# Row maxima of an attention block: their transposition, their store and one activation placed elsewhere

## The chip, the cores and the metric

The kernel runs on one core of one Trainium2 chip. The metric is the device time of one execution in microseconds (us); lower is better. The core has five engines with an instruction queue each: TensorE (PE, matrix products, results in PSUM; its weight loads are listed apart as PEld), VectorE (DVE), ScalarE (ACT), GpSimd (POOL) and SyncE (SP, which here only issues transfers, DMAs). A queue is worked off strictly in order: while an instruction waits for its operands, everything behind it on that engine waits too.

## What is computed

One transformer block on 2048 tokens of width 576: an attention with 32 heads of width 18 and a sliding window of 256 keys, then a shifted mixing layer and an MLP of inner width 4608. The change touches only the attention stage; there the output projection and the two normalizations that follow it are computed as well.

```python
h = layernorm(x) * (1 + ca) + sa
q, k, v = heads(h @ wqkv)                      # 32 heads of 18
scores = where(mask, q @ k.T * 18 ** -0.5, -1e9)   # mask: 0 <= i - j < 256
p = softmax(scores)
x = x + ga * ((p @ v) @ wo)
h = layernorm(x) * (1 + cb) + sb
x = x + gb * B(h)                              # B begins with layernorm(h) @ w1
```

## The kernel before

**Units.** The attention stage works in 32 units n = 0..31. Unit n belongs to 512 queries (group g = n // 8) and to two pairs of heads (j = 0, 1); its queries lie in one of four buffers `QD`, its keys in one of three buffers `KD`. Every unit passes two stations:

- *Maxima.* `mx` (L519 to L525) multiplies the queries with the keys of their window, on PE, in eight blocks of two 320-wide pieces; `red` (L534 to L541) takes the negative maximum of each row, on DVE, into `m`. When all eight blocks are through, `mtr` (L543) transposes `m` on PE into a PSUM tile `mt`, `mev` (L547) copies it to SBUF as `ms` on ACT, and `mst` (L551) stores it by two small DMAs into rows 108 and 109 of the unit's query buffer. From then on the query buffer carries the maxima as two more rows, and the next station subtracts them inside its matrix product.
- *Scores.* About one unit later `xm` (L568, L570) computes the scores X on PE, ten tiles a unit (`X{n}_{j}_{k}`), and `ex` (L585) takes the exponential on ACT into P. Each unit therefore needs its two rows of maxima before its first X tile.

After every second unit comes the *value burst* `av` (L607): 208 small matrix products on PE, without a break, for a pair of units u. Its two results in PSUM are copied by ACT (`avs`, L612), transposed by PE (`ot`, L617) and divided by DVE (L624, L625). From unit 12 on, `wotile` weaves the output projection of one 128-token tile t into each pair of units: `wo` on PE (L692), a normalization on DVE and POOL (`ln1`, `ln2`), and at its end `ln2n` (L713), one activation on ACT that writes the normalized rows `xn`. Three stores by SP follow (`st1`, `st2`, `st3`: `xp`, `hbd`, `xnd`).

**PSUM banks.** Tiles carry a tag that names their bank. X tiles alternate between the banks s0 and s1; `av` and `ot` use s2 and s3; the `mx` blocks alternate between m0 and m1. A tile can be written only when the last reader of the tile before it in the same bank is done. The transposed maxima `mt` use s3.

**Order.** Nothing is scheduled automatically. Every step is entered with a time by `at(time, function)`, where `tm(h)` turns units into time (one unit is 13 of those), and at the end all steps are sorted by that time and issued; each engine's queue is the sorted list of the steps that use it. So a smaller number puts a step further ahead in its engine's queue, and the number has no other meaning. The steps that matter here stand in `wotile` (`ln2n` at h + 2.05) and in the loop over units (`mtr` at n + 1.16 for even n and n + 1.47 for odd n, `mev` .005 and `mst` .006 later). The burst `av` of the units 2u and 2u + 1 has the time 2u + 4.10, `avs` 2u + 4.41, `ot` 2u + 4.51.

**Queues of DMAs.** All large transfers are issued by SP. In the attention stage these are, for each unit, three loads for QD and three for KD, and for each pair of units the loads `or`, `xr` and V and the stores `od`, `xp`, `hbd`, `xnd`. Only the stores of the maxima are issued by ACT.

Of the kernel before, what the change touches and what calls it, by code (L numbers as in the profile page):

```python
# [8 lines left out]
F32 = mybir.dt.float32  # L9
# [10 lines left out]
P = 128  # L20
# [13 lines left out]
class Kern:  # L34
# [34 lines left out]
    def at(self, t, f, *a):  # L69
        self.ev.append((t, (lambda: f(*a)) if a else f))  # L70
# [382 lines left out]
    def attention(self, t1, t2, TA, HU, LX=2.05):  # L453
        nc, at, ps = self.nc, self.at, self.ps
        X, M = {}, self.rowm
        tm = lambda h: TA + HU * h
# [84 lines left out]
                    nc.vector.tensor_reduce(out=m[:, c + s:c + s + 1], in_=pm[:, s, 320 - w:320], axis=mybir.AxisListType.X, op=ALU.max, negate=True)  # L541

        def mtr(n):  # L543
            pt = X["mt", n] = ps.tile([16, P], F32, tag="s3", name=f"mt{n}")
            nc.tensor.transpose(pt, X["m", n], self.ident)

        def mev(n):  # L547
# [3 lines left out]
        def mst(n):  # L551
            ms, Q = X["ms", n], X["Q"][n % 4]
            for r in range(2):
                nc.scalar.dma_start(Q[108 + r:109 + r].bitcast(F32), ms[:, 64 * r:64 * r + 64].bitcast(F32))

        BANKS = [[(0, 0), (5, 320)], [(-2, 0), (1, 192)], [(-4, 0), (2, 64), (6, 384)], [(-3, 0), (3, 128), (7, 448)], [(-1, 0), (4, 256)]]

# [170 lines left out]
        def wotile(t, h, b0=2):  # L728
            at(tm(h - 0.2), orow, t)
            at(tm(h + 0.42), otT, t, b0)  # L730
            at(tm(h + 0.43), otev, t)
            at(tm(h + 0.77), wom, t, 0, b0)
            at(tm(h + 0.92), woe, t, 0)
            at(tm(h + 1.15), wom, t, 1, b0)
            at(tm(h + 1.16), ln1, t, 0)
            at(tm(h + 1.30), woe, t, 1)
            at(tm(h + 1.31), ln1, t, 1)
            at(tm(h + 1.95), st1, t)
            at(tm(h + 1.712), ln1n, t)
            at(tm(h + 1.714), ln2, t)  # L740
            at(tm(h + 2.05), ln2n, t)
            at(tm(h + 2.1), st2, t)
            at(tm(h + 2.35), st3, t)

        N = 32
        for n in range(N):
            at(max(t1 + .5 + n * .01, tm(n - (0.98 if n < 12 else 0.86))), load, n)
            for j in range(2):
                at(max(t1 + .6, tm(n - 0.3 + 0.5 * j)), qs, n, j)
                for bb in range(4):  # L750
                    th = n + (4 * j + bb) / 8
                    at(tm(th), mx, n, j, bb)
                    at(tm(th + .06), red, n, j, bb)
                    if n in (1, 2):
                        at(tm(th + .01), self.warm, 2, "s3")
                at(max(t2 + .01, tm(n + LX - (0.77 if n < 12 else 0.6) + 0.47 * j)), ks, n, j)
                for k in range(5):
                    th = n + LX + (5 * j + k) / 10
                    at(tm(th), xm, n, j, k)
                    at(tm(th + .03), ex, n, j, k)  # L760
            hm = n + (1.47 if n % 2 else 1.16)
            at(tm(hm), mtr, n)
            at(tm(hm + .005), mev, n)
            at(tm(hm + .006), mst, n)
        for u in range(16):
            h = 2 * u + LX + 2
            if u == 15:
# [14 lines left out]
        for t in range(10):  # L782
            wotile(t, 12.4 + 2 * t)
# [618 lines left out]
```

## Time and profile before

| what | value |
|---|---|
| median of 3 runs | 1792.72 us (1791.35 to 1794.88) |
| the profiled execution | 1794.32 us |
| its span, first to last instruction | 1792.5 us |
| mean granted clock of TensorE | 0.982 |
| stage of the projections of q, k and v | up to about 205 us of the span |
| attention stage | about 205 to 665 us |
| mixing layer, then MLP | from about 665 us to the end |

The span is the time between the first and the last instruction of the profiled execution. "Busy" is the time in which an engine works on instructions; "idle before" is the time that it stood still just before an instruction, with the engine and instruction that ended the wait behind the arrow. An idle time matters for the total only if the waiting engine is the one that sets the pace of the stage.

### The profile page before, as it was taken

The page shows a single profiled execution, that of the slowest core. Times are in us where ns is not written, and L with a number is a line of the kernel's source. Part 1 is how long each engine was busy: PE and PEld are TensorE (multiplying, and loading weights), DVE is VectorE, ACT ScalarE, POOL GpSimd, SP SyncE. Part 2 cuts the span into 40 slices and gives each one's busy share as a digit, 9 for nine tenths or more (in the row PEclk, how much of TensorE's full clock was granted, in tenths as well). Part 3 has the DMA queues.
Part 4 walks back from the last instruction along what each step waited for, and adds up shares of the span by engine and source line. Part 5 has one row for each costly group of instructions (what it writes and reads, how often), then busy time and mean ns, then how long its engine had stood idle before and what let it go on. Part 6 is the DMA issues. An engine that isn't in the chain of part 4 may idle for free.

```text
span 1792.5 us, 33622 instructions
## 1 busy us (share of the span) xinstructions
PE 1687.1 (94%) x13369; PEld 1535.6 (86%) x13369; DVE 1103.0 (62%) x1887; ACT 707.3 (39%) x1211; POOL 898.8 (50%) x837
## 2 busy tenths in 40 slices
PE   7999998999999989988799999999979999999998
PEld 5888887888989879988588999999878999999997
DVE  6544354666767636666666666666675666666664
ACT  3222144454545554444333433333433333344331
POOL 4222347445454533454766555556644556655550
PEclk9999998999999999999899999999989999999999
DMA  8854553546455446544422222211233211122211
GB/s 257 275 183 154 176 159 103 145 135 172 130 153 163 145 138 204 192 159 141 162 75 63 63 63 62 59 45 52 62 126 96 63 52 49 56 63 62 62 45 53
DMA packets 156499, 206.77 MB, mean 115 GB/s; under 512 B 19316, under 2 KB 87924, under 8 KB 155768
## 3 DMA queue, kind: packets, MB, share of 16 engines
q1 hardware_dynamic: 153720, 203.19, 36.9%
q8 instruction: 106, 1.74, 0.4%
q10 hardware_dynamic: 2624, 1.45, 0.3%
q14 instruction: 49, 0.40, 0.1%
HBM read 143.76 MB, written 60.56 MB: 114 GB/s over the span
## 4 chain that ended last, share of the span: by engine, by line
PE 73%; DVE 6%; DMA 5%; POOL 5%; issue 4%; ACT 4%; SPq 1%; ACTq 1%; POOLq 0%; DVEq 0%
PE d L1256 24%; PE qk L331 6%; PE X L568 3%; PE v L369 3%; PE mx L519 3%; PE wo L692 3%; PE av L607 3%; PE pg L916 2%; PE X L570 1%; PE w L965 1%; DVE W L1114 1%; DMA wmf<-in_w_mod_dram 1%; DMA or<-od 1%; DMA wf<-in_B_w_dram 1%; ACT avs L612 1%
## 5 line engine op out<-in xcount | busy, mean ns | idle before, releaser
L1256 PE MATMUL d<-W,G 128*128 128x288 f32 x3456 | 507.7, 297 | 12.5 <-DVE acc L1264 9.2
L1256 PEld LDWEIGHTS d<-W,G 128*128 128x128 f32 x3456 | 489.2, 189 | 34.9 <-DVE acc L1264 10.3
L1264 DVE TENSOR_TENSOR acc<-d,acc 128x576 f32<-128x576 f32 x288 | 216.9, 754 | 205.6 <-PE d L1256 203.2
L1094 POOL TENSOR_TENSOR wf<-wf 128x384 f32<-128x384 f32 x140 | 147.0, 1071 | 339.8 <-DMA wf<-in_B_w_dram 333.8
L585 ACT ACTIVATE P<-X 128x512 f32<-128x512 f32 (+4 forms) x320 | 177.8, 572 | 202.3 <-PE X L570 160.8
L537 DVE TENSOR_REDUCE m<-mx 128x2 f32<-128x640 f32 x144 | 117.8, 819 | 109.0 <-PE mx L523 108.5
L568 PE MATMUL X<-QD,KS 128*128 128x64 f32 (+2 forms) x704 | 146.2, 300 | 10.8 <-ACT P L585 9.8
L1106 POOL TENSOR_TENSOR W<-wf,W 128x768 fp32r<-128x768 f32 x70 | 152.9, 2207 | 1.2 <-ACT W L1100 1.2
L519 PE MATMUL mx<-KD,QS 128*128 128x320 f32 (+4 forms) x512 | 144.7, 342 | 7.4 <-DVE m L537 3.2
L1233 DVE TENSOR_TENSOR G<-U,G 128x512 fp32r<-128x512 f32 x108 | 88.5, 819 | 99.0 <-ACT G L1226 99.0
L499 POOL TENSOR_SCALAR QS<-QD,rowm 128x512 fp32r<-128x512 f32 x128 | 87.9, 701 | 111.6 <-DMA QD<-qd 56.4
L1224 ACT ACTIVATE U<-U 128x512 f32<-128x512 f32 x108 | 68.3, 632 | 178.3 <-DVE U L1209 178.2
L1224 ACT ACTIVATE C<-C 128x512 f32<-128x512 f32 x36 | 22.8, 632 | 286.4 <-DVE C L1209 286.4
L568 PEld LDWEIGHTS X<-QD,KS 128*128 128x128 f32 x704 | 108.6, 194 | 19.5 <-ACT P L585 16.1
L331 PE MATMUL qk<-hT,Wqk 128*128 128x512 f32 x462 | 109.3, 396 | 1.2 <-DVE qs L345 1.2
L506 POOL TENSOR_SCALAR KS<-KD,rowm 128x768 fp32r<-128x768 f32 (+1 forms) x128 | 108.5, 863 | 0.0
L1120 POOL TENSOR_TENSOR wf<-wf,gb 128x1152 f32<-128x1152 f32 x35 | 103.4, 2955 | 6.9 <-DMA wf<-in_B_w_dram 6.9
L331 PEld LDWEIGHTS qk<-hT,Wqk 128*128 128x128 f32 x462 | 86.4, 188 | 23.4 <-DVE qs L345 1.6
L519 PEld LDWEIGHTS mx<-KD,QS 128*128 128x128 f32 x512 | 93.5, 194 | 14.1 <-issue 5.3
L1135 POOL TENSOR_TENSOR W<-wf,W 128x1152 fp32r<-128x1152 f32 x35 | 96.8, 2766 | 6.9 <-ACT W L1129 6.9
L1100 ACT CAST W<-wf 128x1152 fp32r<-128x1152 f32 x70 | 90.2, 1318 | 20.5 <-DMA wf<-in_B_w_dram 10.4
L570 PE MATMUL X<-Mk,identr 128*128 128x256 f32 (+2 forms) x320 | 96.6, 302 | 0.0
(787 smaller groups left out, 3211.3 us busy)
## 6 DMA issues: line engine op xcount, KB each, us to landing
wf<-in_B_w_dram SPq DMA_DIRECT2D x35, 576.0 KB
wf<-in_B_w_dram SPq DMA_DIRECT2D x140, 128.0 KB
KD<-kd SPq DMA_DIRECT2D x72, 216.0 KB
QD<-qd SPq DMA_DIRECT2D x96, 144.0 KB
wf<-in_B_w_dram SPq DMA_DIRECT2D x140, 64.0 KB
qd<-qs SPq DMA_DIRECT2D x16, 512.0 KB
kd<-qs SPq DMA_DIRECT2D x16, 512.0 KB
vd<-Vst SPq DMA_DIRECT2D x16, 312.0 KB
```

The source lines that it names most:

```text
L331: nc.tensor.matmul(po, W[:, a, fs], H[:, c, :], start=(n == 0), stop=(n == 13))
L506: nc.gpsimd.tensor_scalar(t[:, b0:, r], src[:, b0:], M[:, 2 + r:3 + r], 0.0, op0=ALU.mult, op1=ALU.add)
L519: nc.tensor.matmul(pm[:, s, 320 - 64 * nb:320], lhs, K[:, j, 64 * (i + 5 - nb):64 * (i + 5)], start=True, stop=merged(n, j, bb))
L537: nc.vector.tensor_reduce(out=m[:, c:c + 2], in_=pm[:, :, 0:320], axis=mybir.AxisListType.X, op=ALU.max, negate=True)
L568: nc.tensor.matmul(px[:, c:c + q1 - q0], K[:, b + 4].rearrange("p r k -> p (r k)"), Q[:, j, q0:q1], start=(i == 0), stop=False)
L570: nc.tensor.matmul(o, self.identr, mv, start=False, stop=True)
L585: nc.scalar.activation(p[:, lo:], X["px", n, j, k][:, lo:], AF.Exp, scale=SCALE)
L1094: nc.gpsimd.tensor_tensor(out=WF[:, o], in0=WF[:, a], in1=WF[:, b], op=ALU.subtract)
L1106: eng.tensor_tensor(out=W[:, s0:s1, 3:5, :], in0=WF[:, 1 + s0:1 + s1, 0:2], in1=W[:, s0:s1, 0:2, :].bitcast(F32), op=ALU.subtract)
L1120: nc.gpsimd.tensor_tensor(out=R4, in0=R4, in1=gb.unsqueeze(1).to_broadcast([P, 2, D]), op=ALU.mult)
L1256: nc.tensor.matmul(po, G[:, g, ta, b, ts], W[:, w, b, cs], start=(n == 0), stop=(n == 5))
L1264: nc.vector.tensor_tensor(out=a, in0=po, in1=a, op=ALU.add)
```

## The change

There are three edits. The transposition `mt` of odd units moves from n + 1.47 to n + 1.105, which is directly behind the value burst (2u + 4.10 with n = 2u + 3), and its PSUM bank becomes s0 instead of s3. The two stores of the maxima are issued by SP instead of ACT, for all units, and .14 behind the transposition instead of .006. The activation `ln2n` moves from h + 2.05 to h + 1.86.

```diff
         def mtr(n):
-            pt = X["mt", n] = ps.tile([16, P], F32, tag="s3", name=f"mt{n}")
+            pt = X["mt", n] = ps.tile([16, P], F32, tag="s0" if n % 2 else "s3", name=f"mt{n}")
             nc.tensor.transpose(pt, X["m", n], self.ident)
...
             for r in range(2):
-                nc.scalar.dma_start(Q[108 + r:109 + r].bitcast(F32), ms[:, 64 * r:64 * r + 64].bitcast(F32))
+                nc.sync.dma_start(Q[108 + r:109 + r].bitcast(F32), ms[:, 64 * r:64 * r + 64].bitcast(F32))
...
-            at(tm(h + 2.05), ln2n, t)
+            at(tm(h + 1.86), ln2n, t)
...
-            hm = n + (1.47 if n % 2 else 1.16)
+            hm = n + (1.105 if n % 2 else 1.16)
             at(tm(hm), mtr, n)
             at(tm(hm + .005), mev, n)
-            at(tm(hm + .006), mst, n)
+            at(tm(hm + .14), mst, n)
```

The order of the queues is shown for unit 17, the same in every odd unit. In the names the first number is the unit (for `av`, `avs` and `ot` the pair u, for `xn` the token tile), and the last is only a buffer number. On ACT, between the exponential of X16_0_1 and that of X16_0_4, there stood before:

```order
L585 ACTIVATE P16_0_1_5601<-X16_0_1_5597 128x512
L585 ACTIVATE P16_0_2_5622<-X16_0_2_5612 128x512
L585 ACTIVATE P16_0_3_5636<-X16_0_3_5626 128x512
L612 COPY avs7_0_5640<-av7_0_5468 128x512
L612 COPY avs7_1_5642<-av7_1_5469 128x512
L717 ACTIVATE xn2_5652<-h2_5574,c2rs_5579 128x576
L549 CAST ms17_5656<-mt17_5654 16x128
L554 DMA QD1_1987<-ms17_5656 1x16x64 x2
L585 ACTIVATE P16_0_4_5660<-X16_0_4_5645 128x512
```

And after the change:

```order
L549 CAST ms17_5576<-mt17_5574 16x128
L585 ACTIVATE P16_0_1_5605<-X16_0_1_5601 128x512
L717 ACTIVATE xn2_5628<-h2_5578,c2rs_5583 128x576
L585 ACTIVATE P16_0_2_5630<-X16_0_2_5618 128x512
L585 ACTIVATE P16_0_3_5644<-X16_0_3_5634 128x512
L612 COPY avs7_0_5648<-av7_0_5468 128x512
L612 COPY avs7_1_5650<-av7_1_5469 128x512
L585 ACTIVATE P16_0_4_5660<-X16_0_4_5653 128x512
```

The copy `ms17` now leads the group, `xn2` has moved ahead of two exponentials and of both `avs`, and the two DMAs are gone from ACT. On PE, at the end of X16_0_4, there stood before:

```order
L568 MATMUL X16_0_4_5645<-QD0_1986,KS16_0_5363 128x256 x2
L570 MATMUL X16_0_4_5645<-Mk_70,identr_64 128x128
L545 MATMUL mt17_5654<-ident_63,m17_5285 16x128
L519 MATMUL mx18_1_0_5662<-KD0_1990,QS18_1_5604 128x320
L523 MATMUL mx18_1_0_5662<-Mq_69,identr_64 128x2x64
L519 MATMUL mx18_1_0_5662<-KD0_1990,QS18_1_5604 128x320
L523 MATMUL mx18_1_0_5662<-Mq_69,identr_64 128x2x64
L617 MATMUL ot7_0_5668<-ident_63,avs7_0_5640 128x128 x4
```

`mt17` has left this place, so that mx18_1_0 directly follows X16_0_4; it now stands here, between the last product of the burst and the next block of maxima:

```order
L607 MATMUL av7_0_5468<-P15_1_3_5441,V7_3832 32x64
L607 MATMUL av7_1_5469<-P15_1_3_5441,V7_3832 32x64
L545 MATMUL mt17_5574<-ident_63,m17_5285 16x128
L519 MATMUL mx18_0_1_5590<-KD0_1990,QS18_0_5410 128x320
L523 MATMUL mx18_0_1_5590<-Mq_69,identr_64 128x2x64
```

On SP, between the loads of two units, the queue after the change is:

```order
L665 DMA xr3_5614<-in_A_x_dram 128x576
L554 DMA QD1_1987<-ms17_5576 1x16x64 x2
L720 DMA xp2_102<-xr2_5138 128x576
L589 DMA V11_5646<-vd11_91 128x624
L723 DMA hbd2_118<-h2_5578 128x576
L726 DMA xnd2_134<-xn2_5628 128x576
L629 DMA od1_97<-o7_5680 128x4x144
L489 DMA QD0_1986<-qd2_74 36x2x512 x3
L493 DMA KD2_1992<-kd2_78 36x2x768 x3
L554 DMA QD2_1988<-ms18_5783 1x16x64 x2
L489 DMA QD1_1987<-qd2_74 36x2x512 x3
```

The two rows of L554 are new on SP; without them the queue before had the same order. The rows of the odd unit 17 stand ahead of the stores `xp2`, `hbd2` and `xnd2`, those of the even unit 18 directly behind the loads of unit 20.

## Prediction

> **What bounds the kernel now.** I read the busy shares first, then PE's work by stretch, then what PE waited for in the attention stage, the only stage that the change touches.
>
> ```profile
> PE 1687.1 (94%) x13369; PEld 1535.6 (86%) x13369; DVE 1103.0 (62%) x1887; ACT 707.3 (39%) x1211; POOL 898.8 (50%) x837
> 400.00:500.00 100.00, 94.83 (x1392) 88.79 (x1391) 69.83 (x135) 48.89 (x91) 48.92 (x74) 1.00 0.54 154
> 1000.00:1792.00 792.00, 773.01 (x4657) 703.97 (x4655) 501.00 (x712) 289.33 (x395) 424.91 (x250) 0.99 0.21 62
> ```
>
> The two lower rows give a stretch, its length, the busy us of PE, PEld, DVE, ACT and POOL, PE's granted clock, the DMA share and GB/s. PE is busy 95 of 100 us in steady attention and 773 of 792 in the MLP; no other engine is over 70. So PE is the bound, and what the change can win is PE's idle time in the attention stage. The view of waits, for PE between 220 and 700 us, lists it (us in total, times, longest):
>
> ```profile
> PE mt L545 <- ACT avs L612: 13.3, 15, 1.3
> PE X L568 <- ACT P L585: 9.8, 19, 2.4
> PE wo L692 <- DVE T L680: 3.9, 1, 3.9
> PE av L607 <- issue: 3.5, 5, 1.9
> PE mx L519 <- DVE m L537: 3.2, 12, 0.7
> ```
>
> The first two are the change's subject. What they look like is seen in the timeline of one period, the one of unit 17 (start, length, engine, instruction, idle time before it and its releaser); ACT first, then PE:
>
> ```profile
> 443.93 1.09 ACT L585 ACTIVATE P<-X 128x512 f32<-128x512 f32 x2 [6.39 <-PE X L570]
> 445.43 0.60 ACT L585 ACTIVATE P<-X 128x512 f32<-128x512 f32 x1 [0.41 <-PE X L570]
> 445.92 1.07 ACT L612 COPY avs<-av 128x512 f32<-128x512 f32 x2
> 446.87 0.89 ACT L717 ACTIVATE xn<-h,c2rs 128x576 f32<-128x576 f32 x1
> 447.64 0.24 ACT L549 CAST ms<-mt 16x128 fp32r<-16x128 f32 x1
> 447.91 1.15 ACTq L554 DMA_DIRECT2D QD<-ms  x2
> 449.11 1.09 ACT L585 ACTIVATE P<-X 128x512 f32<-128x512 f32 x2 [1.23 <-issue]
> ...
> 445.69 0.45 PE L568 MATMUL X<-QD,KS 128*128 128x256 f32 x2
> 445.98 0.22 PE L570 MATMUL X<-Mk,identr 128*128 128x128 f32 x1
> 447.05 0.28 PE L545 MATMUL mt<-ident,m 128*16 128x128 f32 x1 [0.84 <-ACT avs L612]
> 447.14 0.39 PE L519 MATMUL mx<-KD,QS 128*128 128x320 f32 x1
> 447.69 0.60 PE L617 MATMUL ot<-ident,avs 128*128 128x128 f32 x4
> 449.76 0.53 PE L568 MATMUL X<-QD,KS 128*128 128x192 f32 x2 [0.17 <-ACT P L585]
> ```
>
> The odd transposition wants bank s3 and must wait until the second `avs` has emptied it (446.99). Behind it stands `mx`, which needs nothing from ACT. Later X waits 0.17, because ACT issued two DMAs (1.15) before its next exponential.
>
> **The odd transposition.** It adds and removes no work: one small product per odd unit, about 0.1 us on PE (447.05 to 447.14), now behind the burst. There it needs `m`, and DVE's last reduction ahead of the burst's end was over at 437.8; and it needs bank s0, whose reader, the exponential of X16_0_0, ran during the burst (ACT was idle 6.39 us before 443.93). So it should not wait; `ms` falls into ACT's idle time, ahead of the first exponential. The 15 waits, 13.3 us, go.
>
> What is late next? `mx` would start at about 446.05, behind X; it needs bank m0, which DVE frees at 445.71, and `ot` needs `avs` (below). One period is an exception (its two rows stand last):
>
> ```profile
> 437.07 0.69 DVE L535 TENSOR_REDUCE m<-mx 128x2 f32<-128x512 f32 x1
> 444.89 0.82 DVE L537 TENSOR_REDUCE m<-mx 128x2 f32<-128x640 f32 x1 [0.56 <-PE mx L523]
> ...
> 311.41 0.28 PE L545 MATMUL mt<-ident,m 128*16 128x128 f32 x1 [0.99 <-ACT avs L612]
> 312.40 0.39 PE L519 MATMUL mx<-KD,QS 128*128 128x320 f32 x1 [0.71 <-DVE m L537]
> ```
>
> At 312.40 DVE is late too, and the 0.99 would only lengthen the 0.71. I take that period off: −1.0.
>
> **Normalized rows sooner.** The activation's pitch on ACT is 0.77 us (446.87 to 447.64). Ahead of the second exponential it delays that and what follows by 0.77. With 0.1 for the moved product and 0.49 of pitch per exponential (445.43 to 445.92), the second one starts at 444.03 + 0.49 + 0.77 = 445.29 and ends 0.60 later, 445.89. The last X of this half (445.69) reuses that bank and would start at 445.79, so it waits about 0.14: nine periods, −1.3 us. `avs` starts at 446.27 and ends at 447.34; the first `ot` needs its first half at about 446.9, which is just there (bound: 0.05 each, −0.5). What the activation reads is ready in time; the closest of the periods:
>
> ```profile
> 584.51 0.26 POOL L136 TENSOR_SCALAR c7rs<-c7mv,c7rs 128x1 f32<-128x1 f32 x1
> 585.72 1.09 ACT L585 ACTIVATE P<-X 128x512 f32<-128x512 f32 x2 [5.38 <-PE X L570]
> ```
>
> It is ready at 584.77, its new place begins at about 586.3: 1.5 us of cover. If that cover went, every us of delay would hold up the second exponential, and X behind it.
>
> **Stores off ACT.** 64 DMA issues of about 0.6 us leave ACT. For even units from 12 on `wo` (1.9 us on PE) hides them, so nothing is won there. They cost PE time where no `wo` stands, in the early units (the first and the longest of six such waits):
>
> ```profile
> 244.91 0.45 PE L568 MATMUL X<-QD,KS 128*128 128x320 f32 x2 [1.04 <-ACT P L585]
> 295.56 0.44 PE L568 MATMUL X<-QD,KS 128*128 128x320 f32 x2 [2.39 <-ACT P L585]
> ```
>
> The six are 1.04, 1.09, 0.58, 2.39, 1.06 and 1.21, in all 7.4 of the 9.8; in the longest the issue is only 1.2, the rest is a weight cast that waits for POOL. Won: 6.2. Nine waits like the 0.17 at 449.76 go: 1.5. The last 0.8 lie at the end of the stage, where without `mx` ACT sets the pace:
>
> ```profile
> 644.88 0.38 PE L545 MATMUL mt<-ident,m 128*16 128x128 f32 x1 [1.34 <-ACT avs L612]
> 646.95 1.08 ACT L585 ACTIVATE P<-X 128x512 f32<-128x512 f32 x2 [1.25 <-issue]
> ```
>
> That exponential could start at about 645.2, 1.75 sooner, of which 1.34 is in the 13.3: +0.4.
>
> **On SP** the stores are two more issues per unit. No trace row has them there; I bound them below by nothing, since no row shows PE waiting for such a store today, and above by landing late (the slower rival below). The odd ones wait at SP's head for `ms`, until about 443.6; behind them stand `xp`, V, `hbd` and `xnd`, of which only V is read by PE, in the next burst at 465.9. Behind the even ones stand the next unit's loads, which wait for PE anyway (first row). But the even ones themselves come directly behind 1.08 MB of loads (3 × 144 + 3 × 216 KB), and the unit's first X is at 465.45:
>
> ```profile
> SPq L489 <- PE X L570: 118.0, 27, 9.1
> ...
> 454.75 1.29 SPq L493 DMA_DIRECT2D KD<-kd  x3
> 459.00:460.00 1.00, 1.00 (x10) 1.00 (x9) 0.97 (x3) 0.84 (x2) 0.13 (x1) 1.00 0.52 127
> 460.00:461.00 1.00, 1.00 (x10) 1.00 (x9) 0.96 (x3) 0.60 (x1) 0.00 (x0) 1.00 0.04 11
> 465.45 0.40 PE L568 MATMUL X<-QD,KS 128*128 128x320 f32 x2
> ```
>
> The DMA share falls to 0.04 after 460, so even a store that waits for every byte ahead of it has some 4 us left. I take 0.
>
> Here a page speaks against the change. The Trainium skill, "DMA: Bandwidth & Descriptors", section "Queues, rings and completion order", says that SP and ACT own one row of rings each and that the DMA engines take turns between rows by packets, while one row is consumed in order; by it the rows of maxima lose their own lane and wait out the loads. The trace cannot show SP's case; by that rule the landing moves to about 460 or 461, before 465.45, and the sum stays as it is.
>
> **The sum.** 13.3 − 1.0 − 1.3 + 6.2 + 1.5 + 0.4 = 19.1 us. The stages behind start with the attention's results and shift as a whole; the MLP is PE-bound and keeps its length. From the profiled execution, 1794.3 − 19.1 = 1775.2; that execution lies 1.6 above the median of the runs shown, from which it would be 1773.6. I take 1774.5, between the two.
>
> The granted clock is a spread of its own:
>
> ```profile
> 265.00:270.00 5.00, 3.75 (x26) 3.40 (x26) 2.39 (x7) 2.46 (x6) 1.75 (x3) 0.93 0.80 206
> 270.00:275.00 5.00, 5.00 (x23) 5.00 (x23) 2.86 (x7) 2.32 (x5) 3.24 (x4) 0.50 0.08 15
> ```
>
> Half clock came here after waits of only about 1 us, and such stretches may fall elsewhere; I allow ±3 us (5 us at half clock lose 2.5). The skill's page "TensorE: Matmul & The Clock Gate", section "What's actually happening", ties half clock to an idle window of about 3.4 us; no wait near 270 is that long, so here the trace does not bear that rule out, and it changes neither sum nor chance.
>
> **The rivals.**
> - *The wait moves on* (0.17). With `mt` gone, PE stands before `ot` (late `avs`) or `mx` (late DVE), as the 0.71 did at 312.40. For: ten periods now have `xn` ahead of `avs`. Against: 0.05 at most by the sums above. If all ten lost their 0.84, the gain is 19.1 − 8.4 = 10.7: 1783.6; with X waiting somewhat longer, up to 1786.
> - *Nothing that counts* (0.05). A stage behind waits for something that does not shift, or the six early waits and the 13.3 reappear before DVE or POOL. For: `wo` waits 3.9 us for DVE behind attention. Against: POOL is half idle, DVE 30%. About 1791.
> - *Slower: even stores land too late on SP* (0.06). Place: the first X of each even unit, 15 times. It decides at a landing after about 464.5 (465.45 less the period's own gain). The gain is eaten when each lands 1.3 us later than that (15 × 1.3), at 465.8, or 9.8 us after the last load was issued (454.75 + 1.29 = 456.04); 1.7 us late would give 1774.5 + 15 × 1.7 = 1800. Against: idle DMA engines from 460.
> - *The change as summed* (0.72), its own range 1769 to 1780.
>
> Whether a step does what it says is settled by the order: the queues are as shown, so I give that no chance of its own.
>
> **Chances.** A measurement of this kernel tells about 0.2%, 3.6 us, from no change. The summed case and the moved wait are faster (0.89); nothing that counts is the same (0.05); the late stores are slower (0.06). The range 1768 to 1786 holds the first two cases and the clock's spread.
>
> **What would show it.** Right: the wait of `mt` for `avs` is gone from PE's waits, X waiting for P falls from 9.8 to about 3 (the added 0.14s and the rest of the 2.39), the periods of 28 us shrink by about 0.9, and L554 stands in SP's rows. Wrong: a new row in PE's waits with `ot` or X behind ACT, or X behind a DMA into QD; or an attention stage that ends 19 us sooner and an end that doesn't follow.

## The result and the profile after

| | before | after |
|---|---|---|
| median, measured in turns on one chip | 1792.03 us (1790.79 to 1794.88) | 1768.64 us (1766.85 to 1768.80) |
| ratio, 95% interval | | 0.9861 (0.9839 to 0.9884) |
| the profiled execution, its span | 1794.3, 1792.5 us | 1768.65, 1766.8 us |
| ratio when measured again, on another chip | | 0.9878 (0.9859 to 0.9896) |

The kernel is faster, by 23.4 us between the medians; 1774.5 us had been forecast. The busy shares, steady attention by stretch, and PE's waits between 220 and 700 us (us in total, times, longest) are now:

```profile
PE 1677.2 (95%) x13369; PEld 1530.6 (87%) x13369; DVE 1106.2 (63%) x1887; ACT 704.6 (40%) x1211; POOL 898.2 (51%) x837
400.00:500.00 100.00, 98.32 (x1303) 92.84 (x1288) 72.34 (x138) 53.28 (x102) 54.42 (x80) 1.00 0.57 168
PE mx L519 <- DVE m L537: 4.2, 12, 1.7
PE wo L692 <- DVE T L680: 4.0, 1, 4.0
PE av L607 <- issue: 3.2, 3, 2.8
PE w L965 <- DVE xr L696: 2.6, 3, 1.2
PE mx L519 <- issue: 2.2, 10, 0.4
PE X L568 <- ACT P L585: 2.2, 5, 1.0
PE mx L519 <- DVE m L535: 1.4, 2, 1.2
...
PE ot L617 <- ACT avs L612: 0.4, 1, 0.4
...
PE X L568 <- DMA QD<-ms: 0.4, 1, 0.4
```

PE is busy 98.3 instead of 94.8 of 100 us. The odd transposition's wait for `avs` is gone, and X waiting for P has fallen from 9.8 to 2.2. So most of the signs named in the prediction are there. Two rows that it had named as signs of being wrong stand there too, `ot` behind `avs` and X behind a DMA into QD, but each only once and with 0.4 us. What does not fit is the size: periods were to shrink by about 0.9. The even transpositions are the yardstick, since the edits leave them in their place in PE's order; those of the units 12 and 30, after the change (before, they start at 369.63 and 625.60):

```profile
357.96 0.27 PE L545 MATMUL mt<-ident,m 128*16 128x128 f32 x1
600.79 0.27 PE L545 MATMUL mt<-ident,m 128*16 128x128 f32 x1
```

Nine periods lie between them, all at full clock. They took 255.97 us and now take 242.83: 13.1 us, 1.46 a period. The prediction's terms for these nine are 9 × 0.84 + 1.5 − 1.3 = 7.8. Of the 19.1 us, 9.6 were for the units up to 12 (3.4 for five odd transpositions and the 6.2) and 1.7 for the end.

| part of the span | before | after | gain | forecast |
|---|---|---|---|---|
| start to transposition 0 | 225.3 | 226.1 | −0.8 | 0 |
| transposition 0 to 12 | 144.3 | 131.9 | 12.5 | 9.6 |
| transposition 12 to 30 | 256.0 | 242.8 | 13.1 | 7.8 |
| transposition 30 to the end | 1166.9 | 1166.0 | 0.9 | 1.7 |

Below, "the stretch" is always the part from transposition 12 to 30, the third row. It is the steady part and has no half clock, so it can be read to about 1 us.

### The profile page after: what moved, and what is told of

It is laid out like the page before. It is cut to its first block, busy times and chain, and to the rows that moved or that the text cites. A ratio compares the mean times of both kernels' runs of the same rounds, so it can differ in the third digit from the quotient of the medians.

```text
span 1766.8 us, 33658 instructions
## 1 busy us (share of the span) xinstructions
PE 1677.2 (95%) x13369; PEld 1530.6 (87%) x13369; DVE 1106.2 (63%) x1887; ACT 704.6 (40%) x1211; POOL 898.2 (51%) x837
## 4 chain that ended last, share of the span: by engine, by line
PE 80%; DVE 6%; POOL 4%; DMA 4%; issue 3%; ACT 3%; SPq 1%; POOLq 0%; DVEq 0%; ACTq 0%
PE d L1256 24%; PE qk L331 6%; PE mx L519 4%; PE X L568 4%; PE av L607 4%; PE wo L692 3%; PE v L369 3%; PE X L570 2%; PE pg L916 2%; PE w L965 1%; DVE W L1114 1%; PE ot L617 1%; DMA wmf<-in_w_mod_dram 1%; PE mx L523 1%; DMA wf<-in_B_w_dram 1%
## 5 line engine op out<-in xcount | busy, mean ns | idle before, releaser
L537 DVE TENSOR_REDUCE m<-mx 128x2 f32<-128x640 f32 x144 | 117.9, 820 | 91.7 <-PE mx L523 91.1
L1233 DVE TENSOR_TENSOR G<-U,G 128x512 fp32r<-128x512 f32 x108 | 92.8, 859 | 99.4 <-ACT G L1226 99.4
L519 PE MATMUL mx<-KD,QS 128*128 128x320 f32 (+4 forms) x512 | 143.5, 340 | 11.0 <-DVE m L537 4.2
L519 PEld LDWEIGHTS mx<-KD,QS 128*128 128x128 f32 x512 | 93.1, 193 | 16.4 <-issue 7.2
L331 PEld LDWEIGHTS qk<-hT,Wqk 128*128 128x128 f32 x462 | 86.4, 188 | 23.4 <-DVE qs L345 1.6
```

What stands on the lines that cost most here:

```text
L331: nc.tensor.matmul(po, W[:, a, fs], H[:, c, :], start=(n == 0), stop=(n == 13))
L519: nc.tensor.matmul(pm[:, s, 320 - 64 * nb:320], lhs, K[:, j, 64 * (i + 5 - nb):64 * (i + 5)], start=True, stop=merged(n, j, bb))
L537: nc.vector.tensor_reduce(out=m[:, c:c + 2], in_=pm[:, :, 0:320], axis=mybir.AxisListType.X, op=ALU.max, negate=True)
```

## The experiments

One period, start by start, gave the first suspicion. In the row at 449.76 X waits 0.17. The rows around it, before the change (start, length), and behind them the same place after it:

```profile
448.98 0.60 PE L617 MATMUL ot<-ident,avs 128*128 128x128 f32 x4
...
450.25 0.58 PE L568 MATMUL X<-QD,KS 128*128 128x64 f32 x3
450.67 0.34 PE L570 MATMUL X<-Mk,identr 128*128 128x256 f32 x1
```

```profile
433.65 0.60 PE L617 MATMUL ot<-ident,avs 128*128 128x128 f32 x4
434.01 0.51 PE L568 MATMUL X<-QD,KS 128*128 128x192 f32 x2
```

From the start of `ot` to the start of X it was 0.78 us (448.98 to 449.76), and is now 0.36. So 0.42 went, where the row says 0.17: the idle time is counted from the modelled end of `ot` (0.60 long), although the next product normally starts 0.36 after its start. From this come two readings, called "theory pitch" (differences of starts give the size) and "theory idle rows" (the idle rows do, and the surplus has another source) in the expectations. A third, "theory clock", puts the surplus down to fewer stretches at half clock.

| kernel | ratio to before, 95% | the stretch, us |
|---|---|---|
| before; once more | 1 | 256.0; 256.7 |
| stores on SP alone | 0.9970 (0.9956 to 0.9984) | 250.3 |
| odd transposition alone, stores of odd units directly behind | 0.9983 (0.9968 to 0.9998) | 252.3 |
| normalized rows alone | 1.0001 (0.9989 to 1.0013) | 256.8 |
| changed, normalized rows at 2.05 | 0.9884 (0.9864 to 0.9905) | 242.9 |
| changed, normalized rows at 2.10 | 0.9877 (0.9859 to 0.9895) | 242.4 |
| changed; once more | 0.9861; 0.9878 (0.9859 to 0.9896) | 242.8; 241.7 |
| odd transposition alone, stores left at their old place on ACT | 0.9888 (0.9868 to 0.9907) | 242.8 |
| stores of odd units two exponentials later on ACT | 0.9947 (0.9933 to 0.9961) | 251.3 |
| changed, at 2.05, and one block of maxima later | 0.9849 (0.9828 to 0.9870) | 240.3 |

**1. Stores on SP alone**, against the kernel before:

```diff
-                nc.scalar.dma_start(Q[108 + r:109 + r]...
+                nc.sync.dma_start(Q[108 + r:109 + r]...
-            at(tm(hm + .006), mst, n)
+            at(tm(hm + .14), mst, n)
```

> The kernel before with one edit alone: all 64 stores of maxima by SyncE, .14 behind the transposition; the transposition of odd units and the normalized rows stay where they were. Theory pitch (the idle time shown before a matmul counts from the modelled end of the one ahead of it and shows less than the stall; from start to start an X behind ACT's stores loses about .42 + .10 where .17 is shown): nine times .53 = 4.8, the six early waits 6.2 and some .16 more each = 7.2, end of the stage about 1: in all 13 us sooner, ratio .993. Theory idle rows (each edit is worth what the row of the waits says, and the surplus of the whole change has another source): 1.5 + 6.2 + .4 = 8 us, ratio .9955. Theory clock (the surplus is that fewer stretches at half clock occur): 8 us by the sum, with a granted clock that is above that of the kernel before by about .002.

Measured: 0.997, some 5 us, so the total missed both numbers. The stretch is 5.6 us shorter, near theory pitch (4.8) and far from the 1.5 of the idle rows. In one period (the same place):

```profile
442.74 0.28 PE L545 MATMUL mt<-ident,m 128*16 128x128 f32 x1 [0.84 <-ACT avs L612]
...
444.68 0.60 PE L617 MATMUL ot<-ident,avs 128*128 128x128 f32 x4
445.03 0.51 PE L568 MATMUL X<-QD,KS 128*128 128x192 f32 x2
445.38 0.28 PE L570 MATMUL X<-Mk,identr 128*128 128x256 f32 x1
445.49 0.48 PE L568 MATMUL X<-QD,KS 128*128 128x64 f32 x3
445.81 0.33 PE L570 MATMUL X<-Mk,identr 128*128 128x256 f32 x1
```

`ot` to X is 0.35 against 0.78 before, and the second X to its mask product 0.32 against 0.42: two delays behind one late ACT, and only the first has an idle row. What failed in both theories is the early part: the units up to 12, taken without their loss at half clock (as in 6), took 132.1 us against 134.1 and 135.9 in the two traces of before: some 3 us of the 6.2 to 7.2. PE's waits between 225 and 370 us in this run show why:

```profile
PE mx L519 <- POOL QS L499: 3.4, 2, 2.1
PE mx L519 <- DMA KD<-kd: 3.0, 1, 3.0
PE X L568 <- ACT P L585: 1.1, 2, 0.9
```

Before, X waited 7.4 us there for ACT, and `mx` 0.5 for loads and not at all for POOL. So 6.3 us of the early waits went, as forecast, and 5.9 us of others came.

**2. The odd transposition alone**, its stores still on ACT and directly behind its cast:

```diff
-            pt = X["mt", n] = ps.tile([16, P], F32, tag="s3", name=f"mt{n}")
+            pt = X["mt", n] = ps.tile([16, P], F32, tag="s0" if n % 2 else "s3", name=f"mt{n}")
-            hm = n + (1.47 if n % 2 else 1.16)
+            hm = n + (1.105 if n % 2 else 1.16)
```

> The kernel before with one edit alone: the transposition of odd units directly behind the value burst in the other bank; the stores stay on ACT, .006 behind the transposition, and the normalized rows stay at 2.05. The stores of odd units then stand on ACT ahead of the first exponential behind the burst and delay it by some .85, and with it the X that reuses its bank, by about .5. Theory pitch: 14 periods at 1.05 to 1.1 for the transposition and, in the periods with wo, .53 for the X that no longer stands behind the stores, less .5 for the one that now does: about 12 us sooner, ratio .993. Theory idle rows: 13.3 - 1.0 + 1.5 - 7 = 7 us, ratio .996.

Measured: 0.9983, 3 us; the stretch 3.7 us shorter. Both theories expected too much, because both took 0.5 for the X behind the delayed exponential. ACT, then PE, in one of the longer cases:

```profile
434.37 0.26 ACT L549 CAST ms<-mt 16x128 fp32r<-16x128 f32 x1 [4.35 <-PE mt L545]
434.70 1.84 ACTq L554 DMA_DIRECT2D QD<-ms  x2
436.60 0.60 ACT L585 ACTIVATE P<-X 128x512 f32<-128x512 f32 x1 [1.96 <-PE mx L523]
```

```profile
435.98 0.22 PE L523 MATMUL mx<-Mq,identr 128*128 128x128 f32 x1
437.25 0.56 PE L568 MATMUL X<-QD,KS 128*128 128x128 f32 x3 [1.05 <-ACT P L585]
```

From the start of the first issue to the end of the second it took 1.84 here, where 1.15 is usual (each is 0.51 long, and 0.83 lie between them; what the second waited for, no row shows). X starts 1.27 after the product ahead of it, where 0.06 is usual: 1.21 lost. Such an X comes ten times in the stretch, 0.58 to 1.29 behind, in all 8.7 us lost, nearly all that the transposition had won. So two edits that bring 5.6 and 3.7 us alone bring 13 together. A sum of parts could not show that.

**3. The normalized rows alone** (`ln2n` at h + 1.86), **and the changed kernel without that edit** (at h + 2.05).

> The kernel before with one edit alone: the normalized rows at 1.86, ahead of the second exponential; transposition and stores as before. The second avs, for which the odd transposition waits, comes later by what is left of the .77 (about .25), and the last X of the half waits .14, ten times each: 2.5 to 4 us slower, ratio 1.0015 to 1.002, by either theory of the sizes. If the move gained anything by itself (so that it would explain part of the surplus), this run is faster than before.

> The changed kernel without its third edit: the normalized rows stay at 2.05, behind both avs. Theory pitch: the surplus does not come from this edit; without it the X of .14 and the two delays of .05 behind it go in ten periods, so it is 2 to 2.4 us faster than the changed kernel, ratio to the kernel before about .985. Theory idle rows: 1.3 us faster than the changed kernel. If the early normalized rows bring the surplus (a fourth case, since later stages or wo could be served sooner), it is some 5 us slower than the changed kernel, ratio .989.

Measured: 1.0001, the stretch 256.8 (256.0 and 256.7 before); and 0.9884, the stretch 242.9. In the time the edit neither costs nor brings anything that can be seen, in either surrounding. Start by start it does both. In the run with the normalized rows alone, the last X of the half (its product, then X) and the X behind `ot`:

```profile
441.23 0.22 PE L523 MATMUL mx<-Mq,identr 128*128 128x128 f32 x1
441.42 0.50 PE L568 MATMUL X<-QD,KS 128*128 128x256 f32 x2
...
444.81 0.60 PE L617 MATMUL ot<-ident,avs 128*128 128x128 f32 x4
445.32 0.53 PE L568 MATMUL X<-QD,KS 128*128 128x192 f32 x2
```

The last X comes 0.19 behind its product instead of 0.06, in all nine periods: 1.2 us, as forecast. But X comes 0.51 behind `ot` instead of 0.78, and that brings 2.3 us, of which the wait of `mt` and the next X take back 0.9. So nothing is left of the 2.5 to 4 us expected. In the changed kernel the edit loses the same 1.2 and 0.4 more at `ot`, and wins 1.1 at the X behind `ot` and the next one. By the order, this is because the 0.77 us of `xn` no longer lies on ACT between `avs` and the exponential that such an X needs; no run tests that apart. Both runs exclude that this edit is the source of the surplus.

**4. The odd transposition alone, with its stores where they were**, behind both `avs` and the normalized rows. Edit 2, and:

```diff
-            at(tm(hm + .006), mst, n)
+            at(tm(hm + (.371 if n % 2 else .006)), mst, n)
```

> The kernel before with the transposition of odd units directly behind the value burst, but with its two stores left on ACT at the place in the order that they had before (behind both avs and the normalized rows). Theory pitch (sizes from starts, and the transposition alone gained little because its stores went ahead of the first exponential): between the transpositions of the units 12 and 30, where the clock is full, nine periods at .82 to .92 = 7.4 to 8.3 us less than the 256.0 of before, and an X still stands behind the stores, .56 each; the whole about 10 us sooner, ratio .994. Rival store (the transposition gains nothing while any store of maxima is on ACT): as in the run with the edit alone, 252.3 in this stretch, ratio .998.

Measured: 0.9888, the stretch 242.8. That is as short as in the changed kernel, with all stores still on ACT, and more than theory pitch had expected: the X behind the stores lost nothing either. The reason stands in ACT's timeline:

```profile
434.00 0.60 ACT L585 ACTIVATE P<-X 128x512 f32<-128x512 f32 x1 [0.41 <-PE X L570]
434.15 0.51 ACTq L554 DMA_DIRECT2D QD<-ms  x1
434.49 0.58 ACT L612 COPY avs<-av 128x512 f32<-128x512 f32 x1
434.70 0.60 ACTq L554 DMA_DIRECT2D QD<-ms  x1
434.96 0.60 ACT L612 COPY avs<-av 128x512 f32<-128x512 f32 x1
435.43 0.89 ACT L717 ACTIVATE xn<-h,c2rs 128x576 f32<-128x576 f32 x1
436.21 0.60 ACT L585 ACTIVATE P<-X 128x512 f32<-128x512 f32 x1
```

In the program the two issues stand behind both `avs` and `xn`, but they run at 434.15 and 434.70, ahead of them and beside a running exponential; the copies keep their pitch of 0.47 to 0.49 and the next exponential its 0.78. `ms` was ready since 431.9. Before the change the issue had to wait for the cast just ahead of it (447.64), and the exponential behind it started 1.2 us after the issue did (447.91 to 449.11).

The Trainium skill says why this can be, in "Perfetto Trace Analysis", section "Sequencer Loop": an instruction for the engine is put into a queue, where it waits, while a control instruction is executed by the sequencer itself. The rows above agree: the profile lists the two issues under ACTq, the sequencer of ACT. So the strict order in which a queue is worked off, as told at the top, holds in these rows for ACT's computing instructions among themselves, but not for a DMA issue and the computing instructions ahead of it.

**5. The same from the other side:** the kernel before, its odd transposition and its wait left alone, the stores of odd units still on ACT but two exponentials behind the cast.

```diff
-            at(tm(hm + .006), mst, n)
+            at(tm(hm + (.12 if n % 2 else .006)), mst, n)
```

> The kernel before with one edit alone: the two stores of odd units stay on ACT, but stand two exponentials behind the cast that writes their data (.12 behind the transposition instead of .006); the odd transposition stays where it was, so its wait for avs stays. Theory sequencer (a DMA issue costs ACT time only where it must itself wait for the instruction just ahead of it; otherwise it is issued while queued work still runs): the X behind the stores no longer waits, about .6 a period, so the stretch between the transpositions of the units 12 and 30 is 250 to 251 us against 256.0 before, as with the stores on SyncE (250.3), though no DMA has left ACT. Theory issue time (1.15 us of ACT are lost wherever the two issues stand): the stall only moves to a later exponential, and the stretch stays at 255 to 257.

Measured: the stretch 251.3, as the first theory had it; ratio 0.9947 (run 1: 0.9970; the intervals just overlap). One period:

```profile
441.64 0.24 ACT L549 CAST ms<-mt 16x128 fp32r<-16x128 f32 x1
441.78 0.58 ACT L585 ACTIVATE P<-X 128x512 f32<-128x512 f32 x1
442.70 0.60 ACT L585 ACTIVATE P<-X 128x512 f32<-128x512 f32 x1 [0.34 <-PE X L570]
442.77 1.16 ACTq L554 DMA_DIRECT2D QD<-ms  x2
443.99 0.60 ACT L585 ACTIVATE P<-X 128x512 f32<-128x512 f32 x1 [0.68 <-PE X L570]
```

The issues still take 1.16, but they begin beside a running exponential, and the profile puts the wait of the exponential behind them down to its X. (It also starts only 0.06 after the issues end, so this row alone would not decide.) On PE, X comes 0.36 behind `ot` in all nine periods, as with the stores on SP; the 1.0 us between this stretch and that of run 1 lies inside the value bursts. So in the steady part, in odd units, the price of the stores was not that ACT issues them, but that they stood directly behind the cast that they wait for.

**6. Yardsticks, and the normalized rows at 2.10.**

> The changed kernel itself once more, beside the three others on one chip, as their yardstick: ratio to the kernel before between .984 and .9884, and 242.8 us between the transpositions of the units 12 and 30. Theory clock (the surplus is a matter of which executions fell on full clock) would have this stretch, which has no half clock in it, at 248 and the rest made up elsewhere.

> The kernel before once more, for a second trace of it: the stretch between the transpositions of the units 12 and 30 within 1 us of 256.0, as in the first; if it is 254 or less, the decomposition of that stretch is no better than its scatter.

> The changed kernel with the normalized rows at 2.10, behind the exponential that follows the second avs. All theories: between the transpositions of the units 12 and 30 within .1 of a period (1 us in all) of the changed kernel's 242.8, since 1.86 and 2.05 differed there by only .1 us in all; the activation finds room on ACT at any of the three places. If its place matters (that exponential's X is waited for at once, or wo or the store behind comes late), it is at least .3 a period, 3 us, longer than 242.8.

Measured: 0.9878 and 241.7; 256.7; 0.9877 and 242.4. The stretch repeats to about 1 us (what differs lies inside the value bursts), the place of the normalized rows does not matter, and theory clock falls for the stretch. The clock does matter ahead of it. The window from 270 to 275 us (columns as in the prediction's windows: the granted clock is the third number from the right), in the second trace of before and then in the first of the changed kernel:

```profile
270.00:275.00 5.00, 4.91 (x155) 4.45 (x154) 1.50 (x5) 1.81 (x4) 4.22 (x6) 1.00 0.55 159
```

```profile
270.00:275.00 5.00, 3.40 (x78) 2.71 (x84) 2.08 (x5) 1.95 (x5) 4.22 (x5) 1.00 0.58 163
```

The first trace of before had 0.50 there, from the same program. PE's busy time times the missing clock, summed over windows of 2 us, gives for the part from transposition 0 to 12: 10.2 us lost of 144.3 and 1.7 of 137.6 in the two traces of before; 5.1 of 131.9 and 5.1 of 134.3 in the two of after. Without it the part took 134.1 and 135.9, then 126.8 and 129.2: a gain of about 7.0 us.

**7. One step more of the same kind:** the changed kernel with `ln2n` at 2.05, and in odd units from 13 on the second block of maxima behind the next X.

```diff
-                    th = n + (4 * j + bb) / 8
+                    th = n + (4 * j + bb) / 8 + (.03 if n % 2 and n > 12 and (j, bb) == (0, 1) else 0)
```

> The changed kernel with the normalized rows at 2.05 and one more step of the same kind: in odd units from 13 on, the second block of maxima (0,1), which now waits for DVE (row .20, from start to start .51 where .06 is usual, so .45 lost), goes behind the next X. Theory pitch: up to .45 a period less, part of it eaten by that X, whose bank is free some .2 later than it then starts: 2 to 4 us less than 242.8 between the transpositions of the units 12 and 30. Theory idle rows: at most .20 a period, less the X's wait of .2, so nothing.

Measured: 0.9849; the stretch 240.3, 1.4 to 2.5 us below the changed kernel and 2.6 below its nearest relative, the one with the normalized rows at 2.05 (242.9): the low end of what theory pitch gave, where theory idle rows gave nothing. Its row `mx L519 <- DVE m L537` has fallen from 4.2 us, 12 times, to:

```profile
PE mx L519 <- DVE m L537: 2.0, 2, 1.5
```

It has the shortest stretch of all; its ratio and that of the changed kernel measured beside it on one chip (0.9878) have intervals that overlap, so the whole time does not settle which is faster.

## Why the prediction was too small

Direction, the mechanism of the transposition and most signs were right; the mechanism of the stores and several sizes were not. But for `mt`, PE's queue holds the same instructions in the same order before and after, so that they can be paired and the distances from start to start compared. In the stretch, in us (gained means before less after):

| place in PE's order | forecast | gained |
|---|---|---|
| `mx` behind X, where `mt` stood | 7.56 | 9.91 |
| the product behind the burst, where `mt` stands now | 0 | −0.30 |
| X behind `ot`, and the next X | 1.5 | 4.46 |
| last X of the half | −1.3 | −1.17 |
| `ot` behind the product ahead of it | 0 | −0.44 |
| inside the value bursts | 0 | 0.56 |
| all else | 0 | 0.12 |
| together | 7.8 | 13.1 |

The 0.56 is scatter: the two traces of before differ by 0.7 inside the bursts, those of after by 1.2. By the prediction's own steps:

- **"The 15 waits, 13.3 us, go": right, but too small.** They are gone. From start to start each was 1.10 in the stretch (1.16 from the mask product at 445.98 to `mx` at 447.14, usually 0.06) where the row shows 0.84. The kernels of runs 5 and 4, in which no store of odd units holds up ACT, differ by 8.5 us with this edit, 0.94 a period, since some small delays of 0.03 to 0.1 come back behind it.
- **"Nine waits like the 0.17 at 449.76 go: 1.5": the step that failed.** With the transposition's wait left in place it measured 4.6 (run 5) to 5.6 us (run 1), against 256.0. The row's idle time leaves out that a product usually starts well before the modelled end of the one ahead of it (0.42 lost, 0.17 shown), and the products behind are late too without an idle row (0.13 more). The size was wrong, and so was the cause: not the 64 issues as such, but their wait for the cast ahead of them. With the transposition early that wait goes by itself (run 4), so moving the stores to SP brought nothing further in the stretch.
- **"Ahead of the second exponential ... −1.3": right as a cost, but a gain was left out.** The delay of the last X is in the trace (0.20 from 431.14 to 431.34 instead of 0.06, −1.17 in all), and so is that of `ot` which the prediction bounded by 0.5 and left out of its sum (−0.44). But the X behind `ot` comes sooner by it (run 3), and the stretch is the same without the edit: 242.9 against 242.8.
- **"Won: 6.2" in the early units: too large.** The part up to transposition 12 was to win 9.6 and won some 7.0 without the clock. Other waits took the places of the old ones, by the changed kernel's timeline:

```profile
271.50 0.27 PE L519 MATMUL mx<-KD,QS 128*128 128x64 f32 x1 [0.72 <-DMA KD<-kd]
...
288.48 0.44 PE L568 MATMUL X<-QD,KS 128*128 128x320 f32 x2 [1.02 <-ACT P L585]
290.82 0.30 PE L519 MATMUL mx<-KD,QS 128*128 128x64 f32 x1 [1.26 <-POOL QS L499]
305.38 0.61 PE L519 MATMUL mx<-KD,QS 128*128 128x320 f32 x1 [1.72 <-DVE m L537]
320.02 0.53 PE L519 MATMUL mx<-KD,QS 128*128 128x320 f32 x2 [1.23 <-DVE m L535]
320.92 0.47 PE L568 MATMUL X<-QD,KS 128*128 128x320 f32 x2 [0.36 <-DMA QD<-ms]
```

  The longest early wait, the 2.39 at 295.56, has become 1.02 for ACT (288.48) and, right behind, 1.26 for POOL (290.82), so nearly nothing of the 1.2 counted there was won. The waits moved on here: to DVE and POOL, which the rivals had named, and to loads, which none had. Run 4, with all stores on ACT and X waiting 6.7 us for ACT in the early units, took 129.1 for this part without the clock, against 126.8 and 129.2 in the two traces of after; so the 6.2 of the stores is not to be seen. How much each edit pays in these units stays open all the same: traces of one kernel differ there by up to 2.4 us without the clock, and by 8.5 us of half clock.
- **End of the stage, 1.7: reached, then partly lost.** The last X starts 26.9 us sooner (656.74 to 629.83) and transposition 30 24.8, so 2.1 were won; behind it the `w` products wait for `xr` 2.6 instead of 1.2 us, and inside the last value burst PE stands still for 2.75 instead of 1.91, with no releaser in the profile.
- **Stores on SP at 0: right for their landing.** PE waited for one of them once, for 0.36 (320.92 above), and the slower rival fell. Whether standing at SP's head they hold up early loads behind them, the runs do not settle.
- **Clock ±3: too narrow for one trace.** The profiled executions of before and after differ by 5.1 us of half clock up to transposition 12 alone (10.2 − 5.1).

So the forecast missed 5.3 us in the steady part (3.0 at the X behind `ot`, 2.35 at the transposition's wait, the rest in small terms and scatter) and overrated the early units by 2.6 us. Of the 25.7 us between the two profiled executions, some 4 came from the clock (25.3 us of half clock in the whole execution before, 20.9 after).

## What to carry to other kernels

Price a stall of TensorE by the difference of starts, against the same place in a period without the stall; the idle row showed less in every case here (0.17 for 0.42, 0.84 for 1.10). A DMA issue on ACT cost nothing here when its data was ready; placed directly behind the instruction that makes its data, it held up the exponential that followed. A step that shows no effect can still cost in one place and win in another, as the normalized rows did. Two waits that feed each other are priced together: a part of the change tried alone can show a fraction of what it brings in company.

## What the hardware showed unexpectedly

On ACT, DMA issues ran ahead of computing instructions that stand in front of them in the program (434.15 and 434.70, ahead of copies at 434.49 and 434.96), and cost nothing there; directly behind their own cast the same two cost ACT 1.2 us. Half clock fell on different places in two traces of one program: 10.2 us were lost between the transpositions 0 and 12 in one and 1.7 in the other, with nothing in the kernel changed.
